# Three edits in the middle of a spectral filter: loads of z in two pairs, two gradient writes four steps apart, two matmul bursts tied to the main products

## The chip, the cores and the metric

The kernel runs on one core of a Trainium2 chip. A core has a matrix engine (TensorE, PE in the profile; its weight loads are PEld), a vector engine (VectorE, DVE), a scalar engine (ScalarE, ACT), GpSimd (POOL) and SyncE (SP), each with its own instruction queue, worked off in order, and 16 DMA engines that all queues share. The metric is the device time of one execution in microseconds (us). The kernel before took 1199.41 us, the median of three runs from 1198.28 to 1201.03.

## The reference

One forward and backward pass of a block that mixes two branches. With x of 2048 rows by 1024 columns and F = 3584:

```python
g = sigmoid((x * gate_w).sum(-1, keepdims=True))
a = irfft2(rfft2(x) * (w_r + 1j * w_i))          # global spectral filter
h = relu(x @ w1 + b1); b = (h * h) @ w2 + b2     # MLP on the same x
out = g * a + (1 - g) * b
out, vjp = jax.vjp(f, A_x, A_w_r, A_w_i, B_w1, B_b1, B_w2, B_b2, gate_w)
return out, *vjp(grad_out)
```

The inputs are bfloat16. Nine arrays are returned: the output and the gradients for x, the two parts of the filter, both MLP weights and biases, and the gate.

## The kernel before, in words

**Two strands.** The main strand is the MLP: its first layer and the back-propagated hidden gradient (`mlp_in`), the weight gradients (`mlp_grads`), and the output with the gradient for x (`Outputs`). The side strand is the spectral filter with its gradient (`first_stage`, `fft_mid`, `fft_out`). Both are Python generators. `spread` (line 1762) draws from the side strand after each step of the main one, at a rate set by hand: beside the units of `mlp_in` 1.5 side steps for each main step (`first_rate`, 1893). What they emit makes the program order.

**Order on the engines.** Instructions run in an order that a planner makes from the program order: going through modelled time, it takes for each engine the earliest instruction in program order whose operands are ready in its model. So a later instruction can overtake one that waits. Where this is not wanted the kernel draws an edge by hand without a semaphore: `after(ins, earlier, NoSync)` (line 249) keeps `ins` behind `earlier` in the queue. `behind(ins, "PE")` (260) ties to a fixed point, `ahead["PE"]`, and `in_turn(ins, "PE")` (263) to `turn["PE"]`, the last instruction that was noted there. Before the change `turn["PE"]` is noted by the chains of the weight gradients (`Block.chain`, 1236) and of the outputs (1538) alone.

**The main strand beside the middle of the FFT.** From about 225 to 455 us the units of `mlp_in` run. A unit makes four 128 by 512 blocks of h with seven chained products of half size (p1 to p7, `Unit.chain`, lines 918 to 920, tiles `ph` and `pZ`, four matmuls each), and between them four chains of eight matmuls (`pd`, line 819) for the hidden gradient of the unit before. ACT copies partial sums out of PSUM (`cu`, `u`, line 924), applies relu (934, 937) and squares (787); DVE joins partial sums (936) and forms the hidden gradient (823). From about 455 us the weight gradients follow (`Block`, tiles `pX`, `pV`, line 1242).

**The middle of the FFT** (`fft_mid`, from 332) has 16 steps m. The first stage has left in `z_scr` the transforms over columns and a part of the transform over rows, for x and for the scaled gradient at once; a step takes the residues m and 16 + m and does, for the left (h = 0) and right (h = 1) half of the columns:

- `inputs`: two DMAs of 128 KB load `z` (two buffers), on ACT's queue (line 404), tied behind a copy (`copied`).
- `mirrored` (425): sum `pm` and difference of the two residues, on DVE.
- `spectra` (434): four matmuls into the bank pair `px`, with the constants `mats[m]` (`ab`).
- `transform` (439 to 441): ACT copies `px` to `x` in three parts, and one edge column.
- `products` (449), `joined` (454, 461): DVE multiplies the spectra by the filter `w`, which POOL lays out in `by_groups` (410 to 416) from the loaded rows `wn`.
- `rows_of` (468): four matmuls `pv` back; `copy_of` (475): ACT copies one half of `pv` to `vc`; `back` (482, 483): DVE forms `pc`, which POOL's queue stores in `y_scr` (485).
- `grads_of_w` (494, 495): DVE forms the filter's gradient `gs`; `grads_out` (499, 504): ACT scales it into `gw` (one buffer for both halves): one write of 128 by 512 and an edge column for each half; after the left half four DMAs on POOL's queue store its rows (509).
- `filters` (390, 394): POOL's queue loads `ab` and `wn` for the step after.

A step yields eight times: (1) px of both halves, x[1], loads of z; (2) x[0]; (3) products of the right half, the gw writes of the step before, w[0]; (4) pv of both halves, the first vc, filter loads; (5) y[1], back of the right half; (6) gs[1], pm[1], the second vc; (7) pm[0], back of the left half; (8) products and y of the left half, w[1].

Of the kernel before, what the change touches and what calls it, by code (L numbers as in the profile page):

```python
# [10 lines left out]
P = 128  # L11
BF16 = mybir.dt.bfloat16
# [129 lines left out]
def kernel(  # L142
# [33 lines left out]
    Q, H, LW, W1 = D // 4, D // 2, g.Df + 1, g.Df  # L176
# [8 lines left out]
    V, mm = nc.vector.tensor_tensor, nc.tensor.matmul  # L185
# [10 lines left out]
    def pool(name, side="left", space=SBUF, stack=None, bufs=1):  # L196
        stack = ExitStack() if stack is None else stack
        kw = {} if space == DRAM else dict(side=side, reuse_waits="tile")
        return stack.enter_context(tc.tile_pool(name=name, bufs=bufs, space=space, **kw)), stack
# [41 lines left out]
    def columns_of(scr, c, h):  # L241
        return scr[:].rearrange("t c r x h l -> c h (r x) t l")[c, h]
# [7 lines left out]
    def after(ins, earlier, wait=mybir.DependencyClass.Sync):  # L250

        if earlier is not None:
            info = mybir.DependencyInfo(wait, mybir.DependencyReason.DATA)
            tc.add_manual_dep(ins.ins, earlier.ins.name, info, reason="paced")


    turn = {"PE": None, "DVE": None, "ACT": None}
    ahead = {"PE": None, "DVE": None}

    def behind(ins, eng):  # L260
        after(ins, ahead[eng], mybir.DependencyClass.NoSync)

    def in_turn(ins, eng):
        after(ins, turn[eng], mybir.DependencyClass.NoSync)
# [68 lines left out]
    def fft_mid(filler):  # L333
        fb, fbs = pool("f2", "right")
        NM, G = R1 // 2, nc.gpsimd
        WL = HW + 2
        lanes = [slice(R2 * n, R2 * (n + 1)) for n in range(2)]
        every = lambda w_, k: w_.rearrange("(q k) l -> k q l", k=R1)[k]
        mats = {}
# [57 lines left out]
        def inputs(m, h, copied=None):  # L397
            z = fb.tile([P, 2, 2, HW], FDT, name="z", tag="z", bufs=2)
            for n, c in enumerate((m, R1 // 2 + m)):
                from_ = columns_of(z_scr, c, h)  # L400
                if copied is None:
                    ld(out=z[:, n], in_=from_)
                else:
                    after(nc.scalar.dma_start(out=z[:, n], in_=from_), copied, mybir.DependencyClass.NoSync)
            return z

        def by_groups(h, wn):

            w = fb.tile([P, 3, WL], BF16, name="w", tag="w", bufs=2)
            G.tensor_copy(  # L410
                out=w[:, 0:2, 0:HW].rearrange("p c (g i) -> p c g i", g=4),
                in_=wn[:, :, h * HW : (h + 1) * HW].rearrange("p c (i g) -> p c g i", g=4),
            )
            if h:
                G.tensor_copy(out=w[:, 0:2, HW], in_=wn[:, :, H])
            G.tensor_scalar(out=w[:, 2, 0 : HW + h], in0=w[:, 1, 0 : HW + h], scalar1=-1.0, scalar2=None, op0=ALU.mult)
            return w
# [12 lines left out]
        def spectra(m, pm):  # L430
            px = fps.tile([P, 2, 2, HW], FP32, name="px", tag="ps2", bufs=2)
            for c in range(2):
                for n in range(2):
                    behind(mm(px[lanes[n], c], lhsT=mats[m][:, 0, n, lanes[c]], rhs=pm[n], start=True, stop=True), "PE")
            return px

        def transform(m, h, px, ex):
            x = fb.tile([P, 3, 2, WL], FDT, name="x", tag="x", bufs=2)
            nc.scalar.copy(out=x[:, 1:3, :, 0:HW], in_=px[:])
            copied = nc.scalar.mul(out=x[:, 0, :, 0:HW], in_=px[:, 1], mul=-1.0)  # L440
            after(nc.scalar.copy(out=x[:, :, :, h * HW], in_=ex[:, m, :, :, h]), copied, mybir.DependencyClass.NoSync)
            return x, copied
# [21 lines left out]
        def rows_of(m, y):  # L464
            pv = fps.tile([P, 2, 2, HW], FP32, name="pv", tag="ps2", bufs=2)
            for c in range(2):
                for n in (1, 0):
                    mm(pv[:, n], lhsT=mats[m][lanes[n], 1, c, :], rhs=y[lanes[n], c], start=c == 0, stop=c == 1)
            return pv

        def copy_of(m, pv):
            if m == 0:
                return None, None
            vc = fb.tile([P, 2, HW], FP32, name="vc", tag="vc")
            return vc, nc.scalar.copy(out=vc[:], in_=pv[:, 1])
# [22 lines left out]
        def grads_out(m, h, gs, gw, done):  # L498
            main = nc.scalar.mul(  # L499
                out=gw[:, :, h * HW : (h + 1) * HW].rearrange("p c (i g) -> p c i g", g=4),  # L500
                in_=gs[:, :, 0:HW].rearrange("p c (g i) -> p c i g", g=4), mul=GS,
            )
            after(main, done, mybir.DependencyClass.NoSync)
            edge_ = nc.scalar.mul(out=gw[:, :, h * H], in_=gs[:, :, h * HW], mul=0.5 * GS)  # L504
            after(edge_, main, mybir.DependencyClass.NoSync)
            if h == 0:
                for c_, dst_w in enumerate((out_2, out_3)):
                    for n, k in enumerate(pair_of(m, R1)):
                        st(out=every(dst_w, k), in_=gw[lanes[n], c_, 0:W1])  # L509
# [3 lines left out]
        z = {1: inputs(0, 1)}  # L513
# [4 lines left out]
        ex = edges_through(ams)  # L518
# [4 lines left out]
        pm = {h: mirrored(0, z[h]) for h in (1, 0)}  # L523
        x, y, gs, was = {}, {}, {}, None
        yield
        for m in range(NM):
            more = m + 1 < NM
            px = {h: spectra(m, pm[h]) for h in (1, 0)}
            if m:
                gs[0], _ = grads_of_w(0, x[0])  # L530
            x[1], copied = transform(m, 1, px[1], ex)
            if more:
                z = {h: inputs(m + 1, h, copied) for h in (1, 0)}
            yield
            x[0], done = transform(m, 0, px[0], ex)
            yield
            tt = products(1, x[1], w[1])
            if m:
                gw = fb.tile([P, 2, LW], BF16, name="gw", tag="gw")
                for h in (1, 0):  # L540
                    grads_out(m - 1, h, gs[h], gw, done)
            w[0] = by_groups(0, wn[m])
            yield
            if m:
                pv = {h: rows_of(m - 1, y[h]) for h in (1, 0)}
                vc = copy_of(m - 1, pv[1])
            if more:
                wn[m + 1] = filters(m + 1)
            yield
            eh = fb.tile([P, 2, 2], FDT, name="eh", tag="eh")  # L550
            y[1] = joined(1, tt, eh)
            if m:
                back(m - 1, 1, pv[1], vc)
            yield
            gs[1], summed = grads_of_w(1, x[1])
            if more:
                pm = {1: mirrored(m + 1, z[1], summed)}
            if m:
                vc = copy_of(m - 1, pv[0])
            yield  # L560
            if more:
                pm[0] = mirrored(m + 1, z[0])
            if m:
                back(m - 1, 0, pv[0], vc)
            yield
            tt = products(0, x[0], w[0])
            y[0] = joined(0, tt, eh)
            if more:
                w[1] = by_groups(1, wn[m + 1])
            yield  # L570
        gs[0], _ = grads_of_w(0, x[0])
        yield
        gw = fb.tile([P, 2, LW], BF16, name="gw", tag="gw")
        for h in (1, 0):
            pv = rows_of(NM - 1, y[h])
            vc = copy_of(NM - 1, pv)
            yield
            back(NM - 1, h, pv, vc)
            grads_out(NM - 1, h, gs[h], gw, vc[1])
            yield  # L580
        fbs.close()

# [179 lines left out]
    def mlp_in():  # L762
# [52 lines left out]
        def grads(fc, sb, ss, rT, dhT):  # L815
            w_ = w2T[fc // FGC]
            pd = d_bank("pd")
            for ec in range(DC):
                mm(  # L819
                    pd[:], lhsT=w_[:, ec, fc % FGC * P : (fc % FGC + 1) * P], rhs=dbT[:, ec, ss],  # L820
                    start=(ec == 0), stop=(ec == DC - 1),
                )
            return STT(  # L823
                out=dhT, in0=pd[:], scalar=2.0, in1=rT, op0=ALU.mult, op1=ALU.mult,
                accum_out=gb1part[:, fc, sb : sb + 1],
            )
# [52 lines left out]
        KH = DC // 2  # L879
# [33 lines left out]
        class Unit:  # L913
# [3 lines left out]

            def chain(self, acc, lhs, rhs, start):
                for t in range(KH):
                    mm(acc[:], lhsT=lhs[:, t, :], rhs=rhs[:, t, :], start=start and t == 0, stop=t == KH - 1, skip_group_check=True)  # L920

            def copied(self, tag):
                t_ = wb.tile([P, SW], FP32, name=tag, tag=tag, bufs=1)
# [162 lines left out]
        more = [(LAST, s, c) for c in range(2) for s in range(2)]  # L1086
# [867 lines left out]
```

## Time and profile before

| | |
|---|---|
| median of three runs | 1199.41 us |
| profiled execution | 1203.24 us (its span 1201.2) |
| PE busy | 1180.0 us, 98% of the span |
| DVE, ACT, POOL busy | 891.3, 528.7, 379.8 us |
| TensorE clock granted | 1.00 |
| the middle of the FFT, 225 to 455 us | PE busy 220.59, DVE 191.83, ACT 159.42, POOL 146.15 us |
| the same, 455 to 610 us | PE busy 153.17, DVE 111.97, ACT 61.83, POOL 68.84 us |

How to read it: the time of a row stands in microseconds from the start of the span, then how long it took, the engine, the line of the kernel, the instruction, and the tile written and those read. `x2` says that two like rows stand together. In square brackets is the time the engine stood idle before it, with the instruction whose end released it, or `issue` where the profile shows no releaser. ACTq and SPq are DMA issues on those queues. A row of the window view lists the stretch, its length, and the busy time and number of instructions of PE, PEld, DVE, ACT and POOL, then the granted clock, the share of DMA and GB/s. A row of the wait view has who waited for whom, the time in total, how often, and the longest.

### The profile page before, as it was taken

To read this page: it belongs to the slowest core of one execution; us is meant where nothing else is said; L and a number is where in the kernel's file an instruction comes from. 1 tells how busy PE (TensorE), PEld (TensorE's weight loads), DVE (VectorE), ACT (ScalarE), POOL (GpSimd) and SP (SyncE) were. 2 spreads that over 40 slices of the span, in tenths; PEclk is the share of its full clock that TensorE was granted. 3 is DMA by queue.
4 is the path that set the end of the run, shared out by engine and by line. 5 is a ranking of instruction groups with operands and counts; after the bars stand their busy time and mean duration, and the time that the engine had idled before them with its cause. 6 is when DMAs were issued, how large, how long until landed. Compare 5 with 4: busy or idle time off the path is not lost.

```text
span 1201.2 us, 19492 instructions
## 1 busy us (share of the span) xinstructions
PE 1180.0 (98%) x7275; PEld 640.2 (53%) x7275; DVE 891.3 (74%) x1598; ACT 528.7 (44%) x961; POOL 379.8 (32%) x618
## 2 busy tenths in 40 slices
PE   8999999999989999999999999999999999999998
PEld 5555555443434343444446999998544444444444
DVE  5888887778889797877637666666786677986757
ACT  5678788576676773434323666564201010000000
POOL 0233443656657673554241323321001100000000
PEclk9999999999999999999999999999999999999999
DMA  9997675696979789979896999994889999664530
GB/s 267 283 304 212 188 203 166 202 228 170 209 181 217 229 245 170 191 189 227 194 233 135 234 227 252 241 215 155 263 176 239 246 259 302 188 188 153 180 123 36
DMA packets 329464, 249.84 MB, mean 208 GB/s; under 512 B 187912, under 2 KB 287658, under 8 KB 328858
## 3 DMA queue, kind: packets, MB, share of 16 engines
q1 hardware_dynamic: 268352, 112.12, 44.0%
q0 software_dynamic: 35136, 111.72, 29.6%
q10 hardware_dynamic: 25882, 24.76, 7.2%
q8 instruction: 57, 0.93, 0.3%
q14 instruction: 37, 0.30, 0.1%
HBM read 114.82 MB, written 89.67 MB: 170 GB/s over the span
## 4 chain that ended last, share of the span: by engine, by line
PE 71%; DVE 11%; DMA 8%; ACT 5%; issue 3%; POOL 1%; SPq 1%; ACTq 0%; DVEq 0%; POOLq 0%
PE pX L1242 16%; PE pV L1242 11%; PE pd L819 10%; PE xX L1541 10%; PE ph L920 6%; PE xV L1541 5%; PE xZ L1541 3%; DMA w2left<-in_B_w_dram 2%; DMA w1r_scr<-w2left 2%; PE ph L812 2%; PE pui L325 1%; PE pki L627 1%; DMA odd<-h2T_scr 1%; ACT gw L499 1%; PE pu L325 1%
## 5 line engine op out<-in xcount | busy, mean ns | idle before, releaser
L819 PE MATMUL pd<-dbT,w2T 128*128 128x512 bf16 x896 | 211.4, 379 | 4.7 <-DVE dhT L823 3.2
L819 PEld LDWEIGHTS <-w2T 128*128 128x128 bf16 x896 | 86.2, 98 | 108.5 <-issue 9.7
L1541 PEld LDWEIGHTS <-dS 128*128 128x128 f16 x686 | 66.4, 98 | 79.1 <-issue 3.4
L823 DVE SCALAR_TENSOR_TENSOR dhT<-pd,rT 128x512 bf16<-128x512 f32 x112 | 76.7, 684 | 42.8 <-PE pd L819 42.4
L1592 POOL DMA_DIRECT2D out_dram<-ot x32 | 17.3, 542 | 243.6 <-DVE ot L1648 128.0
L1658 ACT ACTIVATE w2br<-w2br,dsc 128x512 f32<-128x512 bf16 x8 | 5.8, 723 | 174.9 <-DVE ot L1648 143.6
L1258 ACT COPY u<-pX 128x512 f32<-128x512 f32 x56 | 32.8, 586 | 99.9 <-PE pX L1242 94.0
L1541 PE MATMUL xX<-oT,dS 128*128 128x512 f16 x336 | 76.4, 379 | 0.2 <-DVE eR L1570 0.2
L1541 PEld LDWEIGHTS <-odd 128*128 128x128 bf16 (+1 forms) x462 | 44.7, 98 | 52.3 <-DMA odd<-h2T_scr 1.0
L1541 PEld LDWEIGHTS <-even 128*128 128x128 bf16 (+1 forms) x448 | 43.7, 98 | 52.6 <-issue 0.7
L1242 PEld LDWEIGHTS <-T 128*128 128x128 f16 x672 | 64.6, 98 | 7.4 <-issue 0.2
L485 POOL DMA_DIRECT2D y_scr<-pc x64 | 46.1, 721 | 51.7 <-DVE pc L482 34.9
L937 ACT ACTIVATE rT<-rT 128x512 bf16<-128x512 bf16 x69 | 43.5, 631 | 42.5 <-DVE rT L936 42.4
L787 ACT ACTIVATE h2T<-rT 128x1024 bf16<-128x1024 bf16 x56 | 59.6, 1064 | 0.3
L1262 DVE TENSOR_TENSOR whi<-pV,u 128x512 bf16<-128x512 f32 x28 | 19.3, 688 | 48.6 <-ACT u L1258 48.5
L1242 PEld LDWEIGHTS <-S 128*128 128x128 f16 x336 | 32.7, 98 | 40.5 <-DVE S L1174 1.9
L449 DVE TENSOR_TENSOR tt<-x,w 128x1028 f16<-128x1028 f16 (+1 forms) x64 | 41.9, 689 | 11.5 <-issue 5.8
L1242 PEld LDWEIGHTS <-resL 128*128 128x128 bf16 x448 | 43.1, 98 | 4.9
L1242 PEld LDWEIGHTS <-resR 128*128 128x128 f16 (+1 forms) x448 | 43.0, 98 | 4.9 <-issue 0.2
L509 POOL DMA_DIRECT2D out_dram<-gw x64 | 33.8, 534 | 35.5 <-ACT gw L504 25.0
L1262 DVE TENSOR_TENSOR wlo<-pV,u 128x512 bf16<-128x512 f32 x28 | 19.2, 686 | 34.2 <-PE pV L1242 34.1
L1242 PEld LDWEIGHTS <-even 128*128 128x128 bf16 (+1 forms) x256 | 24.6, 98 | 32.7 <-issue 2.1
(382 smaller groups left out, 2784.1 us busy)
## 6 DMA issues: line engine op xcount, KB each, us to landing
h2T_scr<-h2T POOLq DMA_DIRECT2D x28, 512.0 KB, 4.6
dhT_scr<-dhT POOLq DMA_DIRECT2D x28, 512.0 KB, 5.0
y_scr<-pc POOLq DMA_DIRECT2D x64, 128.0 KB, 4.0
ax_scr<-yo POOLq DMA_DIRECT2D x16, 512.0 KB, 5.0
out_dram<-ot POOLq DMA_DIRECT2D x31, 256.0 KB, 3.3
z<-z_scr ACTq DMA_DIRECT2D x60, 128.0 KB, 4.5
out_dram<-whi POOLq DMA_DIRECT2D x28, 256.0 KB, 4.9
out_dram<-wlo POOLq DMA_DIRECT2D x28, 256.0 KB, 4.5
```

What stands on the lines that cost most here:

```text
L449: V(out=tt[:, k, :, :, 0:W], in0=x[:, a : a + 2, :, 0:W], in1=by, op=ALU.mult)
L485: st(out=columns_of(y_scr, c, h), in_=pc[:, n])
L509: st(out=every(dst_w, k), in_=gw[lanes[n], c_, 0:W1])
L787: after(nc.scalar.activation(h2T, rT, ACT.Square), behind_, mybir.DependencyClass.NoSync)
L819: mm(pd[:], lhsT=w_[:, ec, fc % FGC * P : (fc % FGC + 1) * P], rhs=dbT[:, ec, ss], start=(ec == 0), stop=(ec == DC - 1),)
L823: return STT(out=dhT, in0=pd[:], scalar=2.0, in1=rT, op0=ALU.mult, op1=ALU.mult, accum_out=gb1part[:, fc, sb : sb + 1],)
L920: mm(acc[:], lhsT=lhs[:, t, :], rhs=rhs[:, t, :], start=start and t == 0, stop=t == KH - 1, skip_group_check=True)
L937: nc.scalar.activation(rT, rT, ACT.Relu)
L1242: self.mm = mm(out, lhsT=lhs[:, t, m * P : (m + 1) * P], rhs=rhs[:, t, :], start=start and t + a == 0, stop=t == KH - 1, skip_group_check= ...
L1258: turn["ACT"] = nc.scalar.copy(out=t_[:], in_=self.X[:])
L1262: turn["DVE"] = self.added = V(out=self.half(row, j), in0=self.sums(acc), in1=self.sums(t_), op=ALU.add)
L1541: ins = mm(acc, lhsT=lhs[:, fc, :], rhs=rhs[:, fc, :], start=start and fc == 0, stop=fc == KH - 1 and bias is None, skip_group_check=True,)
```

## The change

The loads of z for the next step are issued in two pairs: the right half's behind the copies of x[1], as before, and the left half's behind the copies of x[0], one yield later. The gw writes of one step are no longer emitted together in the third part of the next step: the right one (with the allocation of gw) is emitted at the end of its own step, tied behind the second vc copy, and the left one, with the four stores, in the fourth part of the next step behind the first vc copy, tied to the last copy of x[0]. The first matmul of each px and of each pv is tied behind `turn["PE"]`, which is now also noted by the chains of `mlp_in`.

```diff
@@ spectra, rows_of
-                    behind(mm(px[lanes[n], c], ...), "PE")
+                    one = mm(px[lanes[n], c], ...)
+                    behind(one, "PE")
+                    if c + n == 0:
+                        in_turn(one, "PE")
...
-                    mm(pv[:, n], ...)
+                    one = mm(pv[:, n], ...)
+                    if c == 0 and n:
+                        in_turn(one, "PE")
@@ fft_mid, the loop over m
             x[1], copied = transform(m, 1, px[1], ex)
             if more:
-                z = {h: inputs(m + 1, h, copied) for h in (1, 0)}
+                z = {1: inputs(m + 1, 1, copied)}
             yield
-            x[0], done = transform(m, 0, px[0], ex)
+            x[0], copied = transform(m, 0, px[0], ex)
+            if more:
+                z[0] = inputs(m + 1, 0, copied)
             yield
             tt = products(1, x[1], w[1])
-            if m:
-                gw = fb.tile([P, 2, LW], BF16, name="gw", tag="gw")
-                for h in (1, 0):
-                    grads_out(m - 1, h, gs[h], gw, done)
             w[0] = by_groups(0, wn[m])
             yield
             if m:
                 pv = {h: rows_of(m - 1, y[h]) for h in (1, 0)}
                 vc = copy_of(m - 1, pv[1])
+                grads_out(m - 1, 0, gs[0], gw, copied)
...
             y[0] = joined(0, tt, eh)
             if more:
                 w[1] = by_groups(1, wn[m + 1])
+            gw = fb.tile([P, 2, LW], BF16, name="gw", tag="gw")
+            grads_out(m, 1, gs[1], gw, vc[1] if m else None)
             yield
         gs[0], _ = grads_of_w(0, x[0])
         yield
-        gw = fb.tile([P, 2, LW], BF16, name="gw", tag="gw")
         for h in (1, 0):
...
-            grads_out(NM - 1, h, gs[h], gw, vc[1])
+            if h == 0:
+                grads_out(NM - 1, 0, gs[0], gw, vc[1])
@@ mlp_in: grads and Unit.chain
-                mm(
+                turn["PE"] = mm(
                     pd[:], lhsT=w_[:, ec, fc % FGC * P : (fc % FGC + 1) * P], rhs=dbT[:, ec, ss],
...
-                    mm(acc[:], lhsT=lhs[:, t, :], rhs=rhs[:, t, :], ...)
+                    turn["PE"] = mm(acc[:], lhsT=lhs[:, t, :], rhs=rhs[:, t, :], ...)
```

More of the change, by code (lines that the diff above doesn't have):

```diff
@@ L433, in spectra @@
                 for n in range(2):
-                    behind(mm(px[lanes[n], c], lhsT=mats[m][:, 0, n, lanes[c]], rhs=pm[n], start=True, stop=True), "PE")
+                    one = mm(px[lanes[n], c], lhsT=mats[m][:, 0, n, lanes[c]], rhs=pm[n], start=True, stop=True)
+                    behind(one, "PE")
+                    if c + n == 0:
+                        in_turn(one, "PE")
             return px
@@ L467, in rows_of @@
                 for n in (1, 0):
-                    mm(pv[:, n], lhsT=mats[m][lanes[n], 1, c, :], rhs=y[lanes[n], c], start=c == 0, stop=c == 1)
+                    one = mm(pv[:, n], lhsT=mats[m][lanes[n], 1, c, :], rhs=y[lanes[n], c], start=c == 0, stop=c == 1)
+                    if c == 0 and n:
+                        in_turn(one, "PE")
             return pv
@@ L919, in chain @@
                 for t in range(KH):
-                    mm(acc[:], lhsT=lhs[:, t, :], rhs=rhs[:, t, :], start=start and t == 0, stop=t == KH - 1, skip_group_check=True)
+                    turn["PE"] = mm(
+                        acc[:], lhsT=lhs[:, t, :], rhs=rhs[:, t, :], start=start and t == 0, stop=t == KH - 1,
+                        skip_group_check=True,
+                    )
             def copied(self, tag):
```

## The prediction

> **What bounds the kernel now.** I read the engine totals first, then the windows by stage, then what TensorE (PE) waits for inside the stage that the change touches, and last the timeline around single waits.
>
> ```profile
> PE 1180.0 (98%) x7275; PEld 640.2 (53%) x7275; DVE 891.3 (74%) x1598; ACT 528.7 (44%) x961; POOL 379.8 (32%) x618
> ...
> 225.00:455.00 230.00, 220.59 (x1073) 93.23 (x1071) 191.83 (x417) 159.42 (x285) 146.15 (x226) 1.00 0.80 204
> 455.00:610.00 155.00, 153.17 (x738) 66.24 (x736) 111.97 (x173) 61.83 (x119) 68.84 (x105) 1.00 0.92 201
> ...
> PE ph L920 <- ACT u L924: 3.3, 3, 1.3
> PE pd L819 <- DVE dhT L823: 3.2, 4, 1.1
> PE pd L819 <- DVE rT L936: 1.0, 1, 1.0
> PE ph L920 <- ACT rT L934: 0.9, 2, 0.7
> ```
>
> PE is the bound: 98% busy, full clock. The change can only win where PE stands still. The middle of the FFT runs from 225 to 610 us. Up to 455 us, beside the first layers' products, PE idles 9.4 of 230 us and DVE is 83% busy; after 455 us, beside the weight gradients, PE idles 1.8 of 155 us, so little can be won there. The four wait lines (window 225 to 455) say who is late. A listed wait is shorter than the real delay, since each 512-column matmul is drawn 0.38 us long but follows its neighbour after 0.216 us; I use start-to-start delays below.
>
> One step of the FFT takes 21 us, and three steps make four main units, so the picture repeats every 63 us. Here is the place of the largest wait, second of three:
>
> ```profile
> 350.06 0.89 ACTq L404 DMA_DIRECT2D z<-z_scr  x2
> 350.59 0.58 ACT L440 ACTIVATE x<-px 128x512 f16<-128x512 f32 x1
> ...
> 351.07 1.48 ACTq L404 DMA_DIRECT2D z<-z_scr  x2
> ...
> 352.65 0.59 ACT L924 COPY cu<-ph 128x512 f32<-128x512 f32 x1 [1.37 <-issue]
> ...
> 355.52 0.60 ACT L440 ACTIVATE x<-px 128x512 f16<-128x512 f32 x1
> 356.01 1.10 ACT L499 ACTIVATE gw<-gs 128x512 bf16<-128x512 f16 x1
> ...
> 357.18 1.10 ACT L499 ACTIVATE gw<-gs 128x512 bf16<-128x512 f16 x1
> ...
> 358.17 0.58 ACT L924 COPY u<-ph 128x512 f32<-128x512 f32 x1
> ...
> 358.81 1.02 PE L920 MATMUL ph<-xT,Sw 128*128 128x512 f16 x4 [1.01 <-ACT u L924]
> ```
>
> Two things of the FFT stand on ScalarE's (ACT's) queue ahead of main work: the second pair of z loads holds it idle 1.37 us before the copy cu, and both gw writes hold the copy u until 358.17 although its matmuls had ended by 354.8.
>
> **The change, part by part.** *The gw writes.* One write and its edge take 0.98 + 0.10 us of ACT (start to start). Both now stand between x[0]'s copies and u; after the change the left one (of the step before) comes behind the copy vc, the right one near the step's end. At the three places of this kind PE starts late by 1.17 (294.68), 1.18 (358.81) and 1.48 us (420.41). u would start 2.1 us earlier, more than each delay: 3.83 us gone. In the steps whose burst falls at 304 and 369 us the pair stands ahead of vc instead:
>
> ```profile
> 378.96 0.69 DVE L482 TENSOR_TENSOR pc<-pv,vc 128x512 f16<-128x512 f32 x1 [1.14 <-ACT vc L475]
> ...
> 381.58 1.02 PE L920 MATMUL ph<-xT,w1g 128*128 128x512 bf16 x4 [0.70 <-ACT rT L934]
> ```
>
> vc waits for the pair (376.24 to 378.34), DVE's pc for vc, the next vc for pc, rT L934 for that, PE for rT. Without the pair vc starts near 376.4; DVE gains its 1.14 us, more than PE's 0.87 us at 381.58 and 0.36 us at 316.41: 1.22 us. A like delay of 0.28 us (337.36, behind cu) goes too. Sum: -5.3 us. Late next is DVE, whose queue is nearly full, so I do not count more. GpSimd (POOL) still issues four gw stores a step at 0.53 us; they now pass behind the copies of w (L410), which come earlier, and ahead of the next step's filter loads, where a planner already lets the ready ab load overtake them. Behind 455 us I price all this at nothing: PE's 1.8 us there hold no wait on gw.
>
> *The right write's wait.* gw has one buffer, so this write waits until the step before has stored its rows. Today the writes start 9 to 14 us after those stores have landed; then it is a few at most, since the stores go out in the same step. Lower bound 0: at 300.34 to 302.06 ACT idles, the stores landed at 300.88, the write fits. Upper bound 8.2 us, as the second rival works out. I take 1.0, near the lower end: most holes in ACT's queue lie behind the landing.
>
> *The z loads.* The second pair moves behind x[0]'s copies, 0.9 to 4.5 us later by step (start of L439 less start of the pair). ACT loses the 1.37 us hold; I count no PE time for it, since at 353.33 PE waits for DVE. But this pair can be late:
>
> ```profile
> 319.69 0.42 DVE L425 TENSOR_TENSOR pm<-z 128x512 f16<-128x512 f16 x1 [1.88 <-DMA z<-z_scr]
> ...
> 321.94 1.89 PE L819 MATMUL pd<-dbT,w2T 128*128 128x512 bf16 x8 [1.04 <-DVE rT L936]
> ```
>
> Here 2.2 us of DVE wait (1.88 and 0.34) became 1.2 us of PE delay, a share of 0.55. Bounds: 0 and 6.4 us (first rival). I take 1.0, since a queue that holds two loads instead of four lands sooner.
>
> The Trainium skill, "DMA: Bandwidth & Descriptors", section "Rules for kernel authors", says to issue a DMA early and wait late, which speaks against this edit. By that rule the edit is pure loss, up to the first rival's 6.4 us; the row at 319.69 agrees that lateness reaches PE, the hold of 1.37 us shows the other side.
>
> *The ties on PE.* The first px and pv matmul may not pass the main product last written. In the trace the bursts of eight already stand there; only one pv matmul each at 288.24 and 351.81 ran ahead of its seven, where PE had to wait for DVE anyway. A burst costs about 0.1 us to enter; two fewer splits against two lost fillings: between -0.2 and +0.2 us, taken as 0.
>
> Sum: -5.3 + 1.0 + 1.0 = -3.3 us. The profiled execution took 1203.24 us (span 1201.2 and 2.04 around it), so it would take 1199.9. It stands 3.8 us above the median of 1199.41, which becomes **1196.1 us**.
>
> **Rivals.** *First: the late z pair eats the gain.* The second sum pm stands 0.3 us behind the first on DVE. Today its data land, by their semaphores, only 0.1 to 2.2 us ahead of it in six of eleven steps (at 252.0, 293.0, 320.4, 357.5, 382.0 and 419.5). Moved by 2.4 to 4.5 us they would be late by about 1.0, 1.2, 2.6, 1.9, 2.1 and 2.9 us: 11.7 us on DVE, 6.4 by the share of 0.55. For it: DVE works in order. Against it: the planner may move pm, and loads shorten. Time: 1199.41 - 5.3 + 6.4 = 1200.5, about no change.
>
> *Second, the other side: the right write waits for the stores and blocks ACT.*
>
> ```profile
> 314.74 1.07 POOL L509 DMA_DIRECT2D out_dram<-gw  x2
> 320.85 1.04 POOL L509 DMA_DIRECT2D out_dram<-gw  x2 [5.05 <-DMA wn<-in_A_w_r_dram]
> ...
> DMA to landing us min/median/max: 2.2/5.0/9.3
> ```
>
> (The last line is the view of L509, issue to landing.) The stores of this step landed at 323.96. ACT's first hole after the right half's sums is 319.57 to 321.92. A write put there starts at 323.96 and holds the copy u (322.45) by 3.2 us, PE by 2.6. At 384 to 387 (stores landed 387.50, hole from 385.2) it is 2.0; in the three steps with pv near 273, 336 and 399, where the stores would go out behind vc and so later than now, I put the landing 2 to 3 us behind the hole, 1.2 us for PE each (L934, which frees the bank of the next ph, is 3 us late and has 1.9 to spare at 348.25). Together 8.2 us; it turns into a loss once more than 5.3 of them come. With the z edit at 0: 1199.41 - 5.3 + 8.2 = 1202.3. Against it: the planner sees a landing time too, if perhaps a short one.
>
> The skill's page above, section "Anatomy of one DMA — SWDGE (gpsimd) path", puts such a DMA at 2.0 us plus bytes over 436 GB/s, an estimate of 2.15 us for 64.1 KB. By that figure the write would never wait and this rival is worth 0; the trace does not agree, its median is 5.0 us.
>
> *Third: the change reaches nothing or upsets the rest.* Instructions are ordered by a planner; a new order can leave PE a late product elsewhere. The largest delays in the stage are 1.2 to 1.5 us; four new ones cost 5 us: 1201.1 with half the gain.
>
> **How the numbers follow.** A measurement of this kernel tells about 0.2% (2.4 us) from no change. Chances: forecast 0.47 (own range 1192.0 to 1196.9, from all delays with some DVE relief to half of them), first rival 0.21, second 0.24, third 0.08. So faster 0.47, same 0.21, slower 0.32. The range takes in the first and second rival up to 1203.5 and leaves about 1 in 10 on each side.
>
> **What would show it.** Right: no wait of ph L920 on the copy u behind gw writes, the pair of z issues split around x[0]'s copies, PE idle between 225 and 455 us down from 9.4 to about 6. Wrong: ACT idle ahead of gw L499 by a DMA of out_dram, or DVE's pm by a DMA of z more than the 2.2 us of now, with PE late behind u, cu or rT; or a new wait that no line above names.

## The result, and the profile after

The change makes the kernel slower: 1211.76 us (six runs, 1206.32 to 1219.02) against 1199.89 us for the kernel before in the same comparison, a ratio of 1.0106 with a 95% interval of 1.0068 to 1.0144. The forecast of 1196.1 us had the sign wrong, and the time lies above its range. Two single runs of kernels named below, those of 1220.49 and 1211.75 us, were slow ones; they are left out of the ratios, but stand in the medians and ranges.

The profiled execution took 1211.46 us, with a span of 1209.7 (before: 1203.24 and 1201.2), so 8.5 us of span have to be found (the profiled run of before lay 3.8 us above its median, so the medians are further apart). Engine totals and windows of after; a window row has the stretch, its length, the busy time and number of instructions of PE, PEld, DVE, ACT and POOL, the granted clock, the share of DMA and GB/s:

```profile
PE 1176.0 (97%) x7181; PEld 641.1 (53%) x7275; DVE 889.9 (74%) x1598; ACT 531.0 (44%) x961; POOL 377.1 (31%) x618
...
225.00:455.00 230.00, 210.76 (x1004) 89.37 (x1020) 184.54 (x401) 155.02 (x276) 138.99 (x216) 0.99 0.79 192
455.00:610.00 155.00, 152.84 (x729) 66.66 (x740) 113.08 (x180) 64.82 (x122) 65.99 (x104) 1.00 0.92 201
```

The loss lies in the stretch beside the first layers' products: PE's idle time between 225 and 455 us went from 9.4 to 19.2 us; behind 455 us it went from 1.8 to 2.2. Some of the 9.8 us is not real, since records of matmuls are missing (1004 matmuls against 1020 weight loads; 16 x 0.216 = up to 3.5 us). What every engine did in 230 us is less than before, ACT by 4 us, DVE by 7: all of them waited. For whom, the wait view says (who waited, for whom, us in total, how often, the longest), PE from 225 to 620 us:

```profile
PE pd L825 <- DVE rT L945: 6.0, 2, 5.2
PE ph L926 <- ACT cu L933: 5.9, 7, 1.6
PE ph L926 <- ACT u L933: 5.7, 6, 1.9
```

and ACT and DVE from 225 to 465 us:

```profile
ACT gw L504 <- DMA out_dram<-gw: 27.1, 7, 4.8
...
DVE rT L945 <- ACT cu L933: 21.5, 12, 3.4
...
DVE pm L425 <- DMA z<-z_scr: 6.0, 1, 6.0
```

The first row of ACT is new: in the trace of before, no write of gw waits for anything. Now ACT stands 27.1 us in seven waits in front of the right write until the four stores of the left half have landed. Behind this write in ACT's queue stand the copies cu and u. DVE's rT waits for cu, 21.5 us in place of the 1.9 before (`DVE rT L936 <- ACT cu L924: 1.9, 3, 1.2`), and PE waits for cu, u and rT.

What the prediction saw at 350 to 358 us did happen. In the timeline of after, at the same place:

```profile
348.75 1.08 ACTq L404 DMA_DIRECT2D z<-z_scr  x2
...
352.67 0.37 ACTq L404 DMA_DIRECT2D z<-z_scr  x1
...
353.81 0.37 ACTq L404 DMA_DIRECT2D z<-z_scr  x1
354.22 0.59 ACT L933 COPY u<-ph 128x512 f32<-128x512 f32 x1 [0.20 <-issue]
...
354.86 1.02 PE L926 MATMUL ph<-xT,Sw 128*128 128x512 f16 x4
355.66 0.58 ACT L480 COPY vc<-pv 128x512 f32<-128x512 f32 x1
...
356.13 1.12 ACT L504 ACTIVATE gw<-gs 128x512 bf16<-128x512 f16 x1
```

The loads of z stand in two pairs around the copies of x[0], u runs ahead of the write (now the left one, behind vc), and the next chain ph waits for nothing. The delay of 1.18 us at 358.81 is gone. What came in its place stands elsewhere in the step, where the right write is. The worst place:

```profile
371.64 0.37 ACTq L404 DMA_DIRECT2D z<-z_scr  x1
373.13 0.37 ACTq L404 DMA_DIRECT2D z<-z_scr  x1
...
378.41 1.08 POOL L514 DMA_DIRECT2D out_dram<-gw  x2
...
380.65 0.42 DVE L500 TENSOR_TENSOR gs<-g 128x514 f16<-128x514 f16 x1
...
386.64 1.05 POOL L514 DMA_DIRECT2D out_dram<-gw  x2 [7.16 <-DMA wn<-in_A_w_r_dram]
387.36 0.43 DVE L425 TENSOR_TENSOR pm<-z 128x512 f16<-128x512 f16 x1 [5.96 <-DMA z<-z_scr]
...
388.50 3.57 PE L825 MATMUL pd<-dbT,w2T 128*128 128x512 bf16 x8 [5.20 <-DVE rT L945]
...
392.27 1.09 ACT L504 ACTIVATE gw<-gs 128x512 bf16<-128x512 f16 x1 [3.17 <-DMA out_dram<-gw]
393.36 0.57 ACT L933 COPY u<-ph 128x512 f32<-128x512 f32 x1
...
393.98 1.02 PE L926 MATMUL ph<-dbn,Sw 128*128 128x512 f16 x4 [1.91 <-ACT u L933]
```

Read it in two strands. The second pair of z was issued at 371.64 and 373.13 and landed only near 387; DVE's pm waited 5.96 us, rT behind it was late, and PE stood for 5.20 us. The left half's stores were issued two at 378.41 and two at 386.64, since GpSimd waited 7.16 us in between for an older load of wn; the last landed at 392.12, and 0.15 us later the right write began. The first two were late as well: they landed at 389.69 and 391.44, 11.3 and 12.5 us after their issue. The operand gs of the write had been ready since 381.07. This write held u, and PE lost another 1.91 us.

### The profile page after: what moved, and what is told of

It reads as the page before. It is cut to its first block, busy times and chain, and to the rows that moved or that the text cites. A ratio compares the mean times of both kernels' runs of the same rounds, so it can differ in the third digit from the quotient of the medians.

```text
span 1209.7 us, 19381 instructions
## 1 busy us (share of the span) xinstructions
PE 1176.0 (97%) x7181; PEld 641.1 (53%) x7275; DVE 889.9 (74%) x1598; ACT 531.0 (44%) x961; POOL 377.1 (31%) x618
## 4 chain that ended last, share of the span: by engine, by line
PE 71%; DVE 13%; ACT 6%; DMA 5%; issue 4%; POOL 1%; ACTq 0%; another core or an unknown queue 0%; DVEq 0%; POOLq 0%
PE pX L1251 15%; PE xX L1550 13%; PE pV L1251 11%; PE pd L825 8%; PE xV L1550 6%; PE ph L926 4%; PE xZ L1550 3%; DMA out_dram<-gw 3%; PE ph L818 2%; PE pui L325 1%; DMA wn<-in_A_w_r_dram 1%; PE pki L633 1%; DVE rT L945 1%; DVE dhT L829 1%; PE pt L707 1%
## 5 line engine op out<-in xcount | busy, mean ns | idle before, releaser
L825 PE MATMUL pd<-dbT,w2T 128*128 128x512 bf16 x860 | 208.1, 381 | 8.6 <-DVE rT L945 6.0
L1550 PEld LDWEIGHTS <-even 128*128 128x128 bf16 (+1 forms) x448 | 43.7, 98 | 52.6 <-issue 0.7
L504 ACT ACTIVATE gw<-gs 128x512 bf16<-128x512 f16 x32 | 35.4, 1107 | 37.8 <-DMA out_dram<-gw 28.9
L1271 DVE TENSOR_TENSOR wlo<-pV,u 128x512 bf16<-128x512 f32 x28 | 19.2, 687 | 32.4 <-PE pV L1251 32.3
```

The costliest lines, as they stand in the source:

```text
L504: main = nc.scalar.mul(out=gw[:, :, h * HW : (h + 1) * HW].rearrange("p c (i g) -> p c i g", g=4), in_=gs[:, :, 0:HW].rearrange("p c (g i) ...
L825: turn["PE"] = mm(pd[:], lhsT=w_[:, ec, fc % FGC * P : (fc % FGC + 1) * P], rhs=dbT[:, ec, ss], start=(ec == 0), stop=(ec == DC - 1),)
L1271: turn["DVE"] = self.added = V(out=self.half(row, j), in0=self.sums(acc), in1=self.sums(t_), op=ALU.add)
L1550: ins = mm(acc, lhsT=lhs[:, fc, :], rhs=rhs[:, fc, :], start=start and fc == 0, stop=fc == KH - 1 and bias is None, skip_group_check=True,)
```

## The experiments

Each kernel below was timed beside the kernel before; ratios are to it, with 95% intervals.

**The gradient writes alone.** Of the three edits only this: the right write at the end of its own step, the left one with the stores in the fourth part.

```diff
             tt = products(1, x[1], w[1])
-            if m:
-                gw = fb.tile([P, 2, LW], BF16, name="gw", tag="gw")
-                for h in (1, 0):
-                    grads_out(m - 1, h, gs[h], gw, done)
...
                 vc = copy_of(m - 1, pv[1])
+                grads_out(m - 1, 0, gs[0], gw, done)
...
+            gw = fb.tile([P, 2, LW], BF16, name="gw", tag="gw")
+            grads_out(m, 1, gs[1], gw, vc[1] if m else None)
             yield
```

> The kernel before with the gw edit alone: right write at the end of its own step, left write and stores behind vc, one gw buffer; z loads and the order on PE as before. If the loss of the change comes from the right write waiting on ACT for the stores of the step before: 1207 to 1214 us, and ACT idle ahead of the gw write by a DMA of out_dram for some 25 us in the middle of the FFT. If it comes from the late z pair: no slower than before, 1195 to 1200 us, with little ACT idle there. If it comes from the ties on PE: 1195 to 1200 us too.

Measured: 1209.86 us, ratio 1.0082 (1.0066 to 1.0098). ACT's wait of this kernel from 225 to 460 us:

```profile
ACT gw L499 <- DMA out_dram<-gw: 23.5, 8, 4.8
```

So this edit by itself brings most of the loss, and with it the same wait as in the whole change. DVE's sums pm also wait for z here, 4.8 us against 2.2 before, although the four loads stand together; by this way PE stood for 3.19 us at 387.74.

**The split of z alone, and the ties alone.**

```diff
-                z = {h: inputs(m + 1, h, copied) for h in (1, 0)}
+                z = {1: inputs(m + 1, 1, copied)}
             yield
             x[0], done = transform(m, 0, px[0], ex)
+            if more:
+                z[0] = inputs(m + 1, 0, done)
```

> The kernel before with the z edit alone: the left half's loads behind the copies of x[0]. If the gw wait makes the loss: 1198 to 1201 us. If the late z pair makes it: 1205 to 1212 us, with DVE's pm waiting for DMA z well over 2.2 us in all.

> The kernel before with the ties on PE alone. By the prediction's working it moves two pv matmuls: 1199 to 1201 us. If the ties make the loss, by keeping bursts out of PE's holes: 1205 to 1212 us.

Measured: the split 1199.98 us, ratio 1.0004 (0.9987 to 1.0020), with 3.0 us of waits of pm on z (before: 2.2); the ties 1199.83 us, ratio 0.9997 (0.9988 to 1.0005). Each is nothing when it stands alone.

**No wait for the landing.** To take away what the right write waits for, the four stores read another tile.

```diff
-        def grads_out(m, h, gs, gw, done):
+        def grads_out(m, h, gs, gw, done, rows=None):
...
-                        st(out=every(dst_w, k), in_=gw[lanes[n], c_, 0:W1])
+                        after(st(out=every(dst_w, k), in_=rows[lanes[n], c_, 0:W1]), edge_)
...
-                grads_out(m - 1, 0, gs[0], gw, done)
+                grads_out(m - 1, 0, gs[0], gw, done, wn[m])
```

> The gw edit alone again, but the four stores of a step read the loaded filter rows wn instead of gw, still waiting for the left edge write: the same ACT work in the same order and the same DMAs, but no write of gw waits for a landing. The two filter gradients that it returns are the filter's own rows, not the gradients. If the wait for the stores is the loss: 1195 to 1201 us, and no ACT idle ahead of the gw write by a DMA. If it is the new place of the writes in ACT's queue, wait or not: 1207 to 1212 us, as with the gw edit alone.

Measured: 1198.84 us, ratio 0.9992 (0.9981 to 1.0003), against 1.0082 with the wait: 0.90% of 1199.6, 10.8 us, is what the wait for the landing costs in the gradient edit. ACT waits for no DMA between 225 and 460 us. PE's window row:

```profile
225.00:455.00 230.00, 223.83 (x1076) 95.67 (x1094) 196.06 (x419) 165.02 (x296) 142.29 (x223) 1.00 0.78 205
```

PE's idle time is 6.2 us here. By the two intervals the 10.8 us are uncertain by some 2.3. Two reservations. wn is now held until the stores have read it: GpSimd's loads of wn wait 20.9 us for stores between 225 and 460 us, and its copies into w 21.8 us for loads, so that other work is later. And the planner's order is not quite the same: near 295 and 358 us the right write stands earlier in ACT's queue than in the kernel with the gradient writes alone. So 10.8 us is the price of the wait together with what hangs on it.

**Both writes behind the copy vc.** The prediction's gain, without its new wait: both gw writes and the stores go into the fourth part, so the next write comes a whole step after the stores, as before.

```diff
             tt = products(1, x[1], w[1])
-            if m:
-                gw = fb.tile([P, 2, LW], BF16, name="gw", tag="gw")
-                for h in (1, 0):
-                    grads_out(m - 1, h, gs[h], gw, done)
...
                 vc = copy_of(m - 1, pv[1])
+                gw = fb.tile([P, 2, LW], BF16, name="gw", tag="gw")
+                for h in (1, 0):
+                    grads_out(m - 1, h, gs[h], gw, vc[1] or done)
```

> The kernel before with one edit: both gw writes and the stores move from ahead of the copy u to the fourth part, behind vc; they stay together. No write comes near the landing of stores. If the prediction's gain is real (3.8 us at u and some at vc): 1195 to 1198 us, with PE's wait on u down from 3.3 us. If the gain is not there, since PE's next product is late by as much: 1199 to 1201 us.

Measured: 1194.11 us against 1199.59, ratio 0.9962 (0.9949 to 0.9975): 5.5 us gained. The window row and all that PE waits for from 225 to 460 us:

```profile
225.00:455.00 230.00, 225.91 (x1084) 96.55 (x1104) 193.88 (x422) 162.69 (x291) 148.73 (x229) 1.00 0.77 208
```

```profile
PE ph L919 <- ACT u L923: 2.0, 3, 1.3
PE ph L811 <- ACT rT L933: 0.6, 1, 0.6
PE pd L818 <- DVE dhT L822: 0.3, 1, 0.3
```

PE's idle time fell from 9.4 to 4.1 us. The gain comes near the 5.3 us that the prediction had counted, and a little beyond the 1195 to 1198 us expected here. The three waits on u that the prediction named are gone; the 2.0 us on u that are left stand at other places (the longest at 336.82, where the pair of writes now stands ahead of u).

**The same with z in two pairs, and with the ties too.** First the split of z as above, then also the ties of px and pv: the three edits of the change, with the right write in another place.

> The same as both writes behind vc, with the z pairs split as in the change. If the late z pair costs in an order that is otherwise good: 1 to 4 us more than without it, and more spread between runs. If the hold that it takes off ACT is worth something: 0.5 to 2 us less.

> Both gw writes and the stores behind the first vc copy, z in two pairs, and the ties of px and pv on TensorE: the three edits of the change, with the right write one stage later. If the ties do nothing (alone they gave a ratio of 0.9997): 1192.2 us as without them, within 1 us either way, with no wait of the sum pm on z. If the ties are what spread the version with the late right write from 1197 to 1220 us: over 1195 us here, with TensorE idle more than the 3.9 us of 230 that it has without them.

Measured: 1192.18 us, ratio 0.9945 (0.9932 to 0.9958), and with the ties 1191.8 us, ratio 0.9942 (0.9925 to 0.9960). The two can't be told apart; both are faster than the kernel before and than the changed one. The intervals with and without the split (0.9962) overlap, so the split's own part, some 2 us, is not settled. There is no wait of pm on z, and the windows of the version without the ties are:

```profile
225.00:455.00 230.00, 226.13 (x1092) 97.12 (x1113) 194.36 (x426) 164.73 (x293) 148.24 (x229) 1.00 0.78 209
455.00:610.00 155.00, 152.47 (x724) 66.47 (x735) 108.53 (x163) 60.20 (x114) 70.09 (x109) 1.00 0.90 203
```

**The right write later.** The changed kernel, with the right write put back into the third part of the next step (where the stores of the step before have long landed); the left write, the stores, the split and the ties stay.

```diff
             tt = products(1, x[1], w[1])
+            if m:
+                gw = fb.tile([P, 2, LW], BF16, name="gw", tag="gw")
+                grads_out(m - 1, 1, gs[1], gw, copied)
...
-            gw = fb.tile([P, 2, LW], BF16, name="gw", tag="gw")
-            grads_out(m, 1, gs[1], gw, vc[1] if m else None)
             yield
```

> The kernel after, but the right gw write goes back to the third part of the next step, tied to the last copy of x[0] as before the change; the left write and the stores stay behind vc, and z pairs and ties stay. Then the right write follows the stores of the step before by most of a step. If the wait for the stores makes the loss: 1196 to 1201 us and next to no ACT idle ahead of the gw write by a DMA. If the z pair or the ties make it: 1206 to 1213 us, as the kernel after.

> The kernel after with the right gw write back in the third part of the next step, and now the four z loads together again: left write behind vc and the ties are what is left of the change. If the z pairs made the 2 to 20 us by which single runs of the kernel with the right write back were slow: 1196 to 1199 us with a spread of some 4 us as before. If not: 1202 us and wide again.

> The late right write (third part of the next step) with z in two pairs, but without the ties. With the ties this took 1202.8 us (1197 to 1220), and with the ties but four loads of z together 1196.4. If the late second pair of z is the cause: again 1200 us or more, with a spread of over 10 us and waits of pm on z of some 10 us between 225 and 455 us. If the ties are needed for the loss: 1196 us, waits of pm below 3 us.

Measured: 1202.79 us, ratio 1.0023 (0.9998 to 1.0049), with runs spread from 1196.95 to 1220.49 us; with the four loads of z together 1196.4 us, ratio 0.9974 (0.9964 to 0.9985), runs from 1195.23 to 1198.2; with z split but without the ties 1214.53 us, ratio 1.0118 (1.0093 to 1.0143), runs from 1202.53 to 1217.63. The waits of DVE on z from 225 to 460 us, first with the ties, then without them (the profile of the latter is of its fastest run):

```profile
DVE pm L425 <- DMA z<-z_scr: 12.7, 5, 5.9
```

```profile
DVE pm L425 <- DMA z<-z_scr: 10.7, 3, 5.9
```

With the loads together this row is not there. So here the split of z does cost some 6 us, and by another way than the gradient writes: ACT waits for no store in any of the three. The 1202.79 us fits neither of the two ranges expected for it. The ties are not what costs; why the version without them is 11 us slower than the one with them was not found, since its only profile is that of the run of 1202.53 us.

**The whole change with one part out.** The changed kernel with four loads of z together, and the changed kernel whose stores read wn.

> The changed kernel with the four loads of z together again: the gradient writes and the ties stay. If ScalarE's wait for the landed stores is the whole loss: 1209.9 us, as with the gradient writes alone, some 2 us below the changed kernel, and 20 us or more of waits of the gw write on out_dram. If the split of z has its 6 us here too: 1205 us.

> The changed kernel, whose four stores of a step read the filter's rows wn in place of gw, still behind the left edge write; the two filter gradients returned are the filter's rows. So the right write waits for no store, and the z split and the ties stay. If the wait for the landing is the loss of the whole change: 1198.8 us, as with the gradient writes alone in this form, or below. If the split of z costs on its own: 1201 to 1205 us, with waits of pm on z of 5 us and more between 225 and 455 us.

Measured: with the loads together 1211.29 us, ratio 1.0095 (1.0081 to 1.0109), no different from the whole change (1.0106). With the stores reading wn 1204.43 us, ratio 1.0035 (1.0015 to 1.0055), runs from 1193.66 to 1211.75, where the same without split and ties was 0.9992. So with the landing wait in place the split adds nothing that can be measured, and without it the split and the ties together cost 5 us. (In this kernel the hold on wn is longer too: GpSimd's loads of wn wait 28.1 us for stores between 225 and 460 us, in place of 20.9, and its copies into w 25.1 us for loads; what part of the 5 us that is was not separated.) The timeline of the kernel with the four loads together, at the step shown above, says why:

```profile
383.04 0.43 DVE L425 TENSOR_TENSOR pm<-z 128x512 f16<-128x512 f16 x1 [2.02 <-DMA z<-z_scr]
...
389.47 1.08 ACT L504 ACTIVATE gw<-gs 128x512 bf16<-128x512 f16 x1 [4.68 <-DMA out_dram<-gw]
390.54 0.57 ACT L931 COPY u<-ph 128x512 f32<-128x512 f32 x1
391.16 1.87 PE L924 MATMUL ph<-dbn,Sw 128*128 128x512 f16 x4 [5.10 <-ACT u L931]
```

z came 4 us sooner, and PE stood for 5.10 us all the same, now for u behind the right write. The two delays lie side by side: the one that is longer counts.

And in the kernel whose stores read wn the z loads were late by the most of all, in the step around 310 us:

```profile
297.21 17.50 SPq L183 DMA_TRANSPOSE w2T<-in_B_w_dram  x2
...
305.26 0.37 ACTq L404 DMA_DIRECT2D z<-z_scr  x1
...
306.86 0.37 ACTq L404 DMA_DIRECT2D z<-z_scr  x1
...
314.61 0.41 DVE L425 TENSOR_TENSOR pm<-z 128x512 f16<-128x512 f16 x1
...
326.02 0.43 DVE L425 TENSOR_TENSOR pm<-z 128x512 f16<-128x512 f16 x1 [10.99 <-DMA z<-z_scr]
```

The pair issued from 305.26 on was there only near 326. Its issue falls into the time of the two DMA transposes of w2T on SP's queue, which took 17.50 us to issue here, against 6.31 us in the fast version with z split (`296.61 6.31 SPq L183 DMA_TRANSPOSE w2T<-in_B_w_dram  x2`), where z issued at 305.68 and 307.16 was in time. The waits of pm of over 5 us in the profiles (at 387.36 in after, 321.97 and 322.23 in the late versions with z split, 326.02 here) all lie in the step behind such transposes; waits of 3.3 and 3.4 us near 363.5 in the two late versions do not. That they hold z up is argued from this coincidence; no run moved or left out a transpose.

## Why the prediction was wrong

**The gw writes (-5.3 us): the place was right, the size came out in part by luck, the position was not that of the change.** With both writes behind vc the kernel gained 5.5 us, but not by the parts of the sum: PE's waits on u, which were to go, fell from 3.3 to 2.0 us only, and those on dhT and rT, most of which the sum left out, from 5.1 to 0.9. And the change doesn't put the right write there. Where the change has it, and with no wait for the landing, the ratio was 0.9992, some 1 us of gain, not clear of none (0.9981 to 1.0003). The prediction moved a 1.1 us write to the step's end at no price, with no row for what stands behind it there; up to 4.5 us of the gain are lost by that, or by what the stores of wn hold up in that experiment. The two were not separated. (The version with the right write in the third part, 0.9974, has 3.1 us of the gain.)

**The right write's wait (+1.0, bounds 0 to 8.2): this is the step that failed.** It cost some 10.8 us (8.5 to 13.1 by the intervals of the two kernels that it is the difference of). The reason given for taking a value near the lower end was that "most holes in ACT's queue lie behind the landing". In the trace of after no such hole was used: in each of the eight steps from 302 to 456 us the write starts 0.1 to 0.2 us after the last store of its step has landed, and between 256 and 456 us ACT stood idle for that seven times, by 2.9 to 4.8 us. The prediction looked for holes in the order of before; in the order of after the write stands in the queue where its operand gs is ready, and the landing comes later. The upper bound was too small as well. It counted five places, with PE's delays of 2.6, 2.0 and three of 1.2; there were seven, ACT's mean wait was 27.1 / 7 = 3.9 us, and it reached PE by a way that the bound left out, DVE's rT behind cu (1.9 us before, 21.5 after). The remark against the second rival, that the planner sees a landing time too, if perhaps a short one, did not help: the waiting write was put ahead of cu (256.20, 302.06) or u (392.27) all the same. That it stands earlier in the queue at some places where the stores read wn (near 295 and 358 us in the experiment above) suggests that some landing time is seen, too short a one.

The stores were slow as well. The view of their line in after, issue to landing, over the whole execution:

```profile
DMA to landing us min/median/max: 2.8/5.4/14.7
```

Before it was 2.2, 5.0 and 9.3. The Trainium skill, "DMA: Bandwidth & Descriptors", section "Anatomy of one DMA — SWDGE (gpsimd) path", gives 2.0 us plus bytes over 436 GB/s, an estimate of 2.15 us for 64.1 KB, by which the wait would not exist; the trace disagrees here as it did before.

**The z loads (+1.0, bounds 0 to 6.4): inside the bounds where the split was tested by itself; the single value depends on the neighbours.** Alone 0 (1.0004), in the whole change 0 (1.0106 against 1.0095), with both writes behind vc no loss, with the right write in the third part 6 us (1.0023 against 0.9974). The late version without the ties (1.0118) has no partner with the loads together, so there its cost is open. The first rival happened in the profiled run once, at 387.36. The share of 0.55 by which a wait on z was to reach PE is too low for long waits: of 5.96, 5.86 and 10.99 us of pm's waits (in after, in the version with the late right write, in that whose stores read wn) PE stood for 5.20, 5.21 and 10.18. The reason for the low value, that a queue with two loads lands sooner, is right in the median (4.2 us from issue to landing against 5.4 before, from 225 to 455 us) and wrong where it counts: the longest took 15.0 us in after and 19.1 in the kernel whose stores read wn (before it was 14.0, in the step of the wait at 319.69 that the prediction shows). The Trainium skill's rule on the page just named, "Rules for kernel authors", to issue early and wait late, is borne out by the three versions with the late right write, and not by the split alone.

**The ties (0): right.** 0.9997 alone, and 0.9942 against 0.9945 on top of the fast version.

**The rivals.** The second one is what happened: ACT idle ahead of the right write by a DMA of out_dram, PE late behind u, cu and rT, as the list of signs had it. Its price was too low and its chance (0.24) as well. The prediction had the point from which it decides (5.3 us of wait). The third rival's sum is off: new delays of 5 us against half of the 5.3 us give 1201.8; its 1201.1 is what the whole 3.3 us give.

**The sum once more, by what was measured:** the gradient edit in its position -1.0, the landing wait +10.8, the ties and the split about 0 on top: 1199.4 + 9.8 = 1209.2. The measured 1211.76 lies 2.6 us above; the sum is inside its interval (1208 to 1217 us). This is no separate proof, since the first two terms add up to the gradient edit's own 1.0082; it says that the other two edits need no term.

## What to carry to other kernels

When a write is moved next to a DMA that reads the same buffer, price it by the landing and not by the issue: the wait blocks everything behind it in that engine's queue, and an order that looks free of it in the old trace shows no holes of the new one. Move the write a whole turn behind the store or leave it, as the version did that gained 5.5 us. Delays that lie side by side in one step do not add, so an edit that costs nothing beside a large wait may cost several us once that wait is gone, as the split (with the ties) seems to do here.

## What was not expected of the hardware

**After a long standstill of PE the matmuls that follow ran at half rate.** After 5.20 us the eight pd matmuls at 388.50 in after took 3.57 us in place of the usual 1.89. The timeline of the kernel with the gradient writes alone has a standstill without and one with this:

```profile
387.74 1.89 PE L818 MATMUL pd<-dbT,w2T 128*128 128x512 bf16 x8 [3.19 <-DVE rT L935]
...
393.56 1.87 PE L919 MATMUL ph<-dbn,Sw 128*128 128x512 f16 x4 [3.94 <-ACT u L923]
```

After 3.19 us eight matmuls ran at the full rate, 1.89 us; after 3.94 us four took 1.87 in place of 1.02. In the kernel with the four loads together it was the same after 5.10 us (1.87 for four), and in the late versions after 5.2 and 5.3 us (3.57 for eight). The matmuls start 0.427 us apart and not 0.216; in the six profiles seven to thirteen of them did so after one such standstill, which costs an estimated 1.5 to 2.7 us (0.21 us each) more. The granted clock of the stretch shows it as 0.99 in after. In the kernel before no wait of PE in this stretch is over 1.3 us, and none of the matmuls there runs at half rate. The Trainium skill, "TensorE: Matmul & The Clock Gate", section "Part 1: The HAM clock gate", says that the clock is halved after an idle window of about 3.4 us and is full again after as long a busy one; the standstills of 3.94 us and more, and that of 3.19, agree. A threshold is not shown: in the kernel with the gradient writes alone seven matmuls from 352.46 on, and in that with the split alone eight from 416.56 on, ran at half rate as well, behind waits of 1.73 and 1.88 us only. Records of matmuls are missing at both places, and why the rate fell there is open.

**GpSimd's issues waited for its own older DMAs.** The third store of a step waited 7.16 us for a load of wn that had been issued eight DMAs earlier (5.05 in the kernel before), so that two of the four stores went out 8 us after the other two. That is not the whole reason for the late landing, as the first two landed hardly sooner (391.44 against 392.12). All that was issued from 371 to 379 us was slow: the z load at 371.64 took 15.0 us to land, the four loads of wn from 372.23 on 13.2 to 14.1, these two stores 11.3 and 12.5. Beside them two transposes of w2T were being issued on SP's queue (`361.22 16.55 SPq L183 DMA_TRANSPOSE w2T<-in_B_w_dram  x2`); that they slowed the rest is not shown.
